# Attention feeding a squared-relu layer: the second state@w_in group of batch 0 moved between the second and third h of the first four

## The chip, the cores and the metric

The kernel runs on one core of one Trainium2 chip. A core has a matmul engine (TensorE, PE in the profile; its weight loads are listed apart as PEld), three engines that compute on vectors (VectorE or DVE, ScalarE or ACT, GpSimd or POOL), an engine that issues transfers (SyncE or SP), and 16 DMA engines that move data. Matmuls write to PSUM, a small memory out of which VectorE or ScalarE copies the results. The metric is the device time of one execution in microseconds (us).

## The reference

Cut to what matters. Eight batches of x (8 heads, 512 tokens, 64 numbers each) and of state (8 heads, 32 slots, 64 numbers each) attend to each other both ways. The result, 544 rows of 512 numbers for each batch, goes through a layer with a squared relu.

```python
# per batch and head: x is 512 x 64, state is 32 x 64
a = softmax(x @ state.T / 8)          # over the 32 slots
xread = a @ state                     # 512 x 64
a2 = softmax(state @ x.T / 8)         # over the 512 tokens
sread = a2 @ x                        # 32 x 64
rows = concat([xread, sread])         # heads side by side: 544 x 512 for each batch

h = rows @ w_in                       # w_in 512 x 2048
r = maximum(h, 0)
g = s * (r * r) + b
out = g @ w_out                       # w_out 2048 x 512, float32
```

The kernel doesn't compute xread. Since (a @ state) @ w_in = a @ (state @ w_in), it forms M = state @ w_in for each head (the small product, with 32 rows for each head) and multiplies it with the shares a. The 2048 columns of h are made in 16 blocks of 128, f = 0 to 15. A block h_f is the sum of two matmuls, g = 0 and g = 1, each over four heads with 32 slots, so 128 rows. M itself is made in four column blocks of 512, c = 0 to 3. Block c is needed by h of f = 4c to 4c + 3.

## The kernel before

The parts that the change and the steps of the prediction touch. `...` marks cuts.

```python
NG = 2                                # heads in two sets, g = 0 and 1
psA = ctx.enter_context(tc.tile_pool(name="psA", bufs=2, space=bass.MemoryType.PSUM))
psH = ctx.enter_context(tc.tile_pool(name="psH", bufs=2, space=bass.MemoryType.PSUM))
psO = ctx.enter_context(tc.tile_pool(name="psO", bufs=2, space=bass.MemoryType.PSUM))
...
def att_M(b, c, how):                 # M = state @ w_in, column block c
    ...
    if how == "split":
        two = [psO.tile([P, FC], FP32, tag="o", name=f"Mps_{b}_{c}_{g}") for g in range(NG)]
    ...
    for q in range(NQ):               # a group: eight matmuls
        for g in range(NG):
            mm(
                two[g][32 * q : 32 * q + 32],
                st_of(b, head_of(g, q), g),
                wi[c][64 * g : 64 * g + 64, q, :],
                tp=(64 * g, 32 * q),
            )
    dst = a["M"][:, :, FC * c : FC * c + FC]
    ...
    elif how == "split":
        nc.vector.tensor_copy(dst[:, 0], two[0])
        (nc.vector.tensor_copy if c in (0, 3) else nc.scalar.copy)(dst[:, 1], two[1])
...
def mm1_open(key, ntok, f):           # PSUM for one h
    pool, tag = psH, "h"
    if key == 0 and f % 2 == 1:
        pool, tag = (psA, "att") if f < 8 else (psH, "h")
    return pool.tile([P, ntok], FP32, tag=tag, name=f"h_{key}_{f}")
...
def mm1_close(key, hps, ntok, f):     # the relu out of PSUM, then the square
    ...
    if key == 0 and f in (1, 3, 5):
        nc.vector.tensor_scalar(r16[:, f % 2], hps, 0.0, None, ALU.max)
        ...
    else:
        nc.scalar.activation(r16[:, f % 2], hps, AF.Relu)
    ...
def mm1_x4(b, f0, between):           # the first four h of batch 0
    hs = [mm1_open(b, S, f0 + i) for i in range(4)]
    for g in range(NG):
        for i in range(4):
            mm1_k(b, f0 + i, g, hs[i])
        if g == 0:
            between()
    for i in range(4):
        mm1_close(b, hs[i], S, f0 + i)
...
with tc.manual_schedule(engines={ET.PE, ET.SP, ET.Pool}):
    ...
    load_wi(0)                        # GpSimd issues: w_in in four column blocks
    load_wi(1)
    ...
    load_wi(2)
    ...
    load_x(1)
    load_wi(3)
    for q in range(4):
        load_wo(q)
    nc.gpsimd.dma_start(out=st16[:, 4:, 0, :], in_=st_v[:, 4:, :])
    load_x(2)
    ...
    att_M(0, 0, "split")              # the first group
    att_D(0, [1])
    warm_up(2)
    mm1_x4(0, 0, lambda: att_M(0, 1, "split"))     # the second group is between()
    ...
    b0 = {
        4: [lambda: att_M(0, 2, "split")],
        9: [lambda: att_xT_pe(1, 0), lambda: att_xT_pe(1, 1), behind_xT],
        10: [lambda: att_T(1, [0, 1])],
        11: [
            lambda: att_M(0, 3, "split"),
            lambda: att_M(1, 0, "dve"),
            lambda: att_D(1, [0, 1]),
        ],
        ...
    }
    for f in range(4, NKF):
        mm1_x(0, f)                   # h of f = 4 to 15, one after the other
        for fn in b0.get(f, []):
            fn()
```

The program of TensorE, SyncE and GpSimd stands in the order in which it is written. A scheduler orders VectorE and ScalarE. In later blocks the kernel loads x4 and x5 at the first and the eighth block of h of batch 2, and it does so before and after the change alike.

Of the kernel before, what the change touches and what calls it, by code (L numbers as in the profile page):

```python
# [14 lines left out]
def kernel(  # L15
# [383 lines left out]
    def mm1_open(key, ntok, f):  # L399
# [4 lines that stand above are left out]
# [9 lines left out]
    def mm1_close(key, hps, ntok, f):  # L413
        if f % 2 == 0:
            pool, tag, n = (apool, "ET", 3) if (key, f) == (0, 0) else (rpool, "r", 3)
            R2[key] = pool.tile([P, 2, ntok], FP16, name=f"r_{key}_{f}", tag=tag, bufs=n)
        r16 = R2[key]
        if key == 0 and f in (1, 3, 5):
            nc.vector.tensor_scalar(r16[:, f % 2], hps, 0.0, None, ALU.max)
            G["last"] = nc.cur_bb.bb.instructions[-1]  # L420
        else:
            nc.scalar.activation(r16[:, f % 2], hps, AF.Relu)  # L422
            G["relu"] = nc.cur_bb.bb.instructions[-1]
        if f % 4 == 0:
            G4[key, f // 4] = gpool.tile([P, 4, ntok], FP16, name=f"g_{key}_{f}", tag="g")
        gt = G4[key, f // 4]
        G[key, f] = gt[:, f % 4]
        if key == 1 and f in (3, 5):
            with tc.issue_after(nc.cur_bb.bb.instructions[-1]):
                nc.scalar.square(gt[:, f % 4 - 1 : f % 4 + 1], r16)  # L430
        elif f % 2 == 1:

            def square():
                nc.vector.tensor_mul(gt[:, f % 4 - 1 : f % 4 + 1], r16, r16)  # L434

            if (key, f) in ((0, 1), (0, 3), (0, 7), (0, 9), (1, 11)):
                held.append(square)
                return
            if (key, f) == (0, 5):
                release(1, 1)  # L440
            square()
            G["last"] = nc.cur_bb.bb.instructions[-1]

    def mm1_k(b, f, g, hps):
        a = A[b]
        mm(
            hps,
            a["M"][:, g, P * f : P * f + P],
            a["a4"][:, g, :],
            start=(g == 0),  # L450
            stop=(g == NG - 1),
        )
# [7 lines left out]
    def mm1_x4(b, f0, between):  # L460
        hs = [mm1_open(b, S, f0 + i) for i in range(4)]
        for g in range(NG):
            for i in range(4):
                mm1_k(b, f0 + i, g, hs[i])
            if g == 0:
                between()
        for i in range(4):
            mm1_close(b, hs[i], S, f0 + i)

# [303 lines left out]
    with tc.manual_schedule(engines={ET.PE, ET.SP, ET.Pool}):  # L773
# [72 lines left out]
        att_D(0, [1])  # L846
        warm_up(2)
        mm1_x4(0, 0, lambda: att_M(0, 1, "split"))

        def behind_xT():  # L850
# [226 lines left out]
```

## Time and profile before

| what | before |
|---|---|
| time, median of 3 runs | 206.67 us (206.36 to 210.62) |
| span of the profiled execution | 204.9 us |
| TensorE busy | 197.8 us |
| VectorE busy | 165.7 us |
| ScalarE busy | 127.5 us |
| GpSimd busy | 38.7 us |
| mean granted TensorE clock | 0.998 |

The span runs from the first to the last instruction. Busy time counts the durations of an engine's instructions; matmuls overlap one another in the pipeline, so that TensorE's is not TensorE at its peak. The chain that ended last follows the work back from the last instruction, at each step to what released it. In the timeline a row merges neighbouring instructions of one kind: start, time from the first start to the last end, engine, line of the kernel, operation, output<-input, and their number. A bracket at a row's end gives the idle time of that engine before it and what ended it.

In the start phase, M<-Mps are the copies of the groups, a<-E,R the shares, h<-a,M the blocks of h, and r<-h their relus. Mps<-wi,stT are the groups themselves. The line L70 is a helper through which all matmuls go. The rows are told apart by their tiles.

### The profile page before, as it was taken

The numbers are of one execution on the slowest core, as the hardware profiler recorded it, in microseconds if no ns is written. First come the engines' busy times: TensorE is split into PE (matmuls) and PEld (weight loads), VectorE is DVE, ScalarE is ACT, GpSimd is POOL, SyncE is SP. The second block draws the span as 40 slices with busy tenths as digits, with TensorE's granted clock in tenths as the row PEclk, the third lists the DMA queues.
The fourth block names the chain that finished last, engine by engine and source line by source line (L and its number), as shares of the span: only waits on it lengthen the run. The fifth ranks groups of instructions, "written<-read, shape, count | busy, mean of one in ns | idle before, by whom it ended". The sixth has DMA issues, their size and how long they took to land.

```text
span 204.9 us, 4900 instructions
## 1 busy us (share of the span) xinstructions
PE 197.8 (97%) x1986; PEld 132.9 (65%) x1986; DVE 165.7 (81%) x301; ACT 127.5 (62%) x253; POOL 38.7 (19%) x66
## 2 busy tenths in 40 slices
PE   7889999999999999999999999999999999999992
PEld 2424333667776776677676767676767777788982
DVE  4589878987969985999679976997699786696862
ACT  2569867899476757765776668666867545543100
POOL 5870001232230231023102101120112012100210
PEclk9999999999999999999999999999999999999999
DMA  5999997999989995939882904160416011200143
GB/s 166 229 203 206 206 194 97 191 122 235 172 116 120 150 290 82 194 98 216 110 102 62 233 25 106 51 163 0 102 54 160 3 51 51 101 6 2 61 147 104
DMA packets 46795, 25.52 MB, mean 125 GB/s; under 512 B 31604, under 2 KB 44788, under 8 KB 46772
## 3 DMA queue, kind: packets, MB, share of 16 engines
q0 software_dynamic: 15568, 16.19, 41.1%
q1 hardware_dynamic: 30324, 8.52, 25.5%
q10 hardware_dynamic: 880, 0.49, 0.9%
q8 instruction: 15, 0.25, 0.5%
q14 instruction: 8, 0.07, 0.1%
HBM read 17.30 MB, written 8.91 MB: 128 GB/s over the span
## 4 chain that ended last, share of the span: by engine, by line
PE 87%; DMA 9%; POOL 1%; DVE 1%; SPq 0%; issue 0%
PE h L70 25%; PE oB L70 18%; PE oA L70 12%; PE oC L70 12%; DMA wi<-in_moe_w_in_dram 6%; PE Mps L70 4%; PE o L70 4%; PE h_sr L70 3%; DMA xf<-in_x_dram 3%; PE oB_0b L70 1%; PE V L70 1%; PE oB_sr L70 1%; PE oC_0b L70 1%; PE oA_0b L70 1%; PE oC_sr L70 1%; PE oA_sr L70 1%
## 5 line engine op out<-in xcount | busy, mean ns | idle before, releaser
L422 ACT ACTIVATE r<-h 128x512 f16<-128x512 f32 x125 | 73.4, 602 | 43.9 <-PE h L70 43.9
L70 PE MATMUL h<-a,M 128*128 128x512 f16 x256 | 73.4, 379 | 0.5 <-ACT r L422 0.3
L70 PEld LDWEIGHTS <-s 128*128 128x128 f16 x464 | 44.1, 98 | 14.8
L434 DVE TENSOR_TENSOR g<-r 128x1024 f16<-128x1024 f16 x62 | 41.9, 681 | 12.4 <-ACT r L422 11.9
L70 PEld LDWEIGHTS <-g 128*128 128x128 f16 x392 | 37.2, 98 | 18.6 <-issue 4.1
L70 PE MATMUL oB<-wd,s 128*128 128x256 f16 x224 | 32.8, 272 | 0.0
L70 PE MATMUL oA<-wo,g 128*128 128x256 f16 x224 | 32.5, 273 | 0.0
L70 PEld LDWEIGHTS <-M 128*128 128x128 f16 x256 | 24.4, 98 | 11.4 <-issue 1.4
L626 POOL DMA_DIRECT2D out_dram<-osb x13 | 8.8, 676 | 69.5 <-DVE rt L352 35.3
L314 ACT CAST M<-Mps 128x1024 f16<-128x1024 f32 x20 | 20.1, 1006 | 0.0
L70 PE MATMUL oC<-wd,s 128*128 128x256 f16 (+1 forms) x120 | 16.5, 266 | 0.0
L70 PE MATMUL oB<-wd,g 128*128 128x256 f16 x112 | 15.7, 273 | 0.0
L70 PE MATMUL oC<-wo,s 128*128 128x256 f16 (+1 forms) x120 | 15.4, 266 | 0.0
L626 POOL DMA_DIRECT2D out_dram<-u x7 | 4.7, 678 | 40.7 <-DVE inv L297 26.6
L422 ACT ACTIVATE r_sr<-h_sr 128x256 f16<-128x256 f32 x16 | 6.1, 382 | 7.9 <-PE h_sr L70 6.4
L653 DVE SCALAR_TENSOR_TENSOR u<-oB,s_bc,qa 128x512 f32<-128x512 f32 x7 | 5.2, 748 | 6.3 <-PE oB L70 6.2
L238 ACT ACTIVATE E<-T 128x256 f16<-128x256 f32 x20 | 7.4, 384 | 4.0 <-PE T L70 4.0
L550 DVE TENSOR_TENSOR s<-s,g 128x1024 f16<-128x1024 f16 x14 | 9.6, 685 | 0.2
L70 PE MATMUL h_sr<-srdT,wi 128*128 128x256 f16 x64 | 9.6, 273 | 0.0
L552 DVE TENSOR_TENSOR s<-g,s 128x1024 f16<-128x1024 f16 x14 | 9.6, 683 | 0.0
L548 DVE TENSOR_TENSOR s<-g,g 128x1024 f16<-128x1024 f16 x14 | 9.5, 682 | 0.0
L543 DVE TENSOR_TENSOR s<-g 128x1024 f16<-128x1024 f16 x14 | 9.5, 683 | 0.0
(137 smaller groups left out, 241.3 us busy)
## 6 DMA issues: line engine op xcount, KB each, us to landing
out_dram<-osb POOLq DMA_DIRECT2D x15, 256.0 KB, 4.2
xn<-in_x_dram POOLq DMA_DIRECT2D x7, 512.0 KB, 8.6
wi<-in_moe_w_in_dram POOLq DMA_DIRECT2D x4, 512.0 KB, 9.3
wo<-in_moe_w_out_dram POOLq DMA_DIRECT2D x4, 512.0 KB, 16.4
out_dram<-u POOLq DMA_DIRECT2D x7, 256.0 KB, 2.5
out_dram<-qb POOLq DMA_DIRECT2D x7, 256.0 KB, 3.2
xf<-in_x_dram SPq DMA_DIRECT2D x2, 512.0 KB, 5.0
out_dram<-osb_0b POOLq DMA_DIRECT2D x2, 128.0 KB, 6.1
```

The lines of the kernel that those rows point to most:

```text
L70: return nc.tensor.matmul(out, lhsT, rhs, start=start, stop=stop, tile_position=tp, is_transpose=is_transpose, skip_group_check=True,)
L238: nc.scalar.activation(a["E"][:, g, 256 * m : 256 * m + 256], Ts[m][:, g, :], AF.Exp, scale=scale, accum_out=a["rs"][:, NG * m + g : NG * ...
L314: nc.scalar.copy(dst, ps)
L422: nc.scalar.activation(r16[:, f % 2], hps, AF.Relu)
L434: nc.vector.tensor_mul(gt[:, f % 4 - 1 : f % 4 + 1], r16, r16)
L543: nc.vector.tensor_sub(o, a11, a21)
L548: nc.vector.tensor_add(o, a21, a22)
L550: nc.vector.tensor_sub(o, SQ[b, 1, j], a11)
L552: nc.vector.tensor_sub(o, a12, SQ[b, 2, j])
L626: nc.gpsimd.dma_start(dst[j][:, :, n0 : n0 + NH], osb)
L653: nc.vector.scalar_tensor_tensor(u, acc["B"], s_bc, kept["qa"], ALU.mult, ALU.add)
```

## The change

The first four blocks of h are made in two halves, g = 0 of all four and g = 1 of all four, with the second group of state@w_in between the halves. The change puts this group between the second and the third h of the half g = 0. It is for the copies of column block 1 out of PSUM, which can begin as soon as the group is done and on which h of f = 4 rests. The number of instructions is the same.

```diff
@@ mm1_x4 @@
         for g in range(NG):
             for i in range(4):
                 mm1_k(b, f0 + i, g, hs[i])
-            if g == 0:
-                between()
+                if (g, i) == (0, 1):
+                    between()
         for i in range(4):
             mm1_close(b, hs[i], S, f0 + i)
```

## The prediction

> **What bounds the kernel now.** I read the page first, then the chain that ended last in order of time, then the timeline of 8 to 24 us, then the landing times of single loads. The page says who is the bound on average:
>
> ```profile
> PE 197.8 (97%) x1986; PEld 132.9 (65%) x1986; DVE 165.7 (81%) x301; ACT 127.5 (62%) x253; POOL 38.7 (19%) x66
> ...
> PE 87%; DMA 9%; POOL 1%; DVE 1%; SPq 0%; issue 0%
> ```
>
> TensorE (PE) carries 87% of the chain, a DMA 9%. The changed instructions run near 13 us, in the start phase, so the average doesn't decide; the chain there does. Its pieces (start, length, what):
>
> ```profile
> 8.04 0.83 POOL xn L121
> 8.87 11.92 DMA wi<-in_moe_w_in_dram
> 20.79 0.04 issue
> 20.83 0.48 PE Mps L70 x8
> 21.31 0.61 DVE M L337
> 21.92 0.68 DVE M L338
> ```
>
> From 8.87 to 20.79 the chain is one transfer: the fourth column block of w_in (wi_3), issued at 8.87 and used by the group of products state@w_in that starts at 20.83. No piece of TensorE between 8.87 and 20.83 lies on it. What the change moves stands inside those 11.92 us:
>
> ```profile
> 11.40 0.41 DVE L281 TENSOR_TENSOR a<-E,R 128x512 f16<-128x512 f16 x1
> ...
> 11.73 0.68 DVE L338 CAST M<-Mps 128x512 f16<-128x512 f32 x1
> ...
> 11.97 1.02 PE L70 MATMUL h<-a,M 128*128 128x512 f16 x4
> 12.39 0.42 DVE L281 TENSOR_TENSOR a<-E,R 128x512 f16<-128x512 f16 x1
> ...
> 12.93 0.41 PE L70 MATMUL Mps<-wi,stT 64*32 64x512 f16 x8
> ...
> 13.27 1.04 PE L70 MATMUL h<-a,M 128*128 128x512 f16 x4
> 13.40 0.69 DVE L337 CAST M<-Mps 128x512 f16<-128x512 f32 x1 [0.58 <-PE Mps L70]
> 13.43 0.59 ACT L338 CAST M<-Mps 128x512 f16<-128x512 f32 x1 [1.07 <-PE Mps L70]
> 13.92 1.09 ACT L422 ACTIVATE r<-h 128x512 f16<-128x512 f32 x2
> 14.01 1.28 DVE L419 TENSOR_SCALAR r<-h 128x512 f16<-128x512 f32 x2
> ...
> 14.57 0.59 PE L70 MATMUL h<-a,M 128*128 128x512 f16 x2 [0.26 <-ACT r L422]
> ```
>
> The first line of h (11.97, four matmuls) is the half g=0 of h0 to h3; then comes the group (12.93), then the half g=1 (13.27). The copies of the group out of PSUM (13.40 on VectorE, 13.43 on ScalarE) are idle before it and wait for it. h4 at 14.57 waits for a relu that frees its buffer.
>
> Then the three places where TensorE meets loads:
>
> ```profile
> 15.09 0.11 PEld L70 LDWEIGHTS <-stT 64*32 64x32 f16 x8 [0.42 <-DMA wi<-in_moe_w_in_dram]
> ...
> 17.44 1.04 PEld L70 LDWEIGHTS <-xn 128*128 128x128 f16 x16 [0.17 <-DMA xn<-in_x_dram]
> ...
> 20.83 0.63 PE L70 MATMUL Mps<-wi,stT 64*32 64x512 f16 x16 [0.24 <-DMA wi<-in_moe_w_in_dram]
> ```
>
> The bracket is idle time of that queue and what released it. Issue starts and times to landing give the landings: wi_1 2.95 + 9.2 = 12.15; wi_2 5.36 + 9.3 = 14.66; x_1 7.99 + 9.4 = 17.39; wi_3 8.87 + 11.9 = 20.77. The 0.42 at 15.09 is hardly a wait: the groups at 12.93 and 26.01 show the same 0.42 with "issue" as cause, and the step from the last h (14.78) is 0.31, as at 12.93 (from 12.62).
>
> **What the Trainium skill says.** "PSUM — Partial Sum Buffer", section Engine vs sequencer instructions: matmuls start and complete in program order, ScalarE and VectorE queues are strict FIFO. So a group that waits holds all matmuls behind it. The trace agrees: nothing of TensorE's work behind wi_3 begins before 20.83. "TensorE: Matmul & The Clock Gate", section Back-to-back issue gap: a single warm matmul of 512 columns costs N/2.4 + 2.5, about 216 ns, though a stream could go to some 131. The trace agrees with the first alone: ten h start at 15.43 and the next matmul at 17.60, 0.217 us each. "DMA: Bandwidth & Descriptors", section Two DMAs through the same engine are not ordered: within one queue of an engine, descriptors start in order. The four landings above come in order of issue, 2.5 to 3.4 us apart, agreeing; compute can't pull wi_3 forward.
>
> **The change part by part.** Nothing is added or removed: the sixteen instructions (eight weight loads and eight matmuls) of the second group pass in front of two matmuls, h2 and h3 of g=0. In the built program only TensorE's order differs; VectorE, ScalarE, GpSimd and SyncE keep theirs, and with it every DMA issue keeps its place. Step by step, before to estimated after:
>
> 1. Group: 12.93 becomes 12.19 (start of h1) + 0.30 (step from an h to a group) = 12.49, 0.44 earlier. It may start: wi_1 landed at 12.15, and its second PSUM half is freed by the VectorE copy ending 11.73 + 0.68 = 12.41, plus 0.06 of signalling (the warm-up matmul started at 11.54 after a copy that ended at 11.48) = 12.47. It fits by 0.02 us.
> 2. h2, h3 of g=0: 12.41 and 12.62 become 12.49 + 0.34 = 12.83 and 13.05. The half g=1 starts at 13.05 + 0.22 = 13.27, as now. TensorE's total is unchanged; only order changes.
> 3. Copies: 13.40 and 13.43 become about 12.96 and 12.99. VectorE is free for it at 12.39 + 0.42 = 12.81.
> 4. Relus: ScalarE's first is freed from the copy (which would end at 13.57) and now waits for h0: 13.27 + 0.38 + 0.06 = 13.71 instead of 13.92, a gain of 0.21. VectorE's first waits for h1: 13.49 + 0.38 + 0.05 = 13.92 instead of 14.01, a gain of 0.09; its second needs h3 at 13.92 + 0.38 and VectorE at 13.92 + 0.68 = 14.60, where it was at 14.61.
> 5. h4 waits for ScalarE's first relu: 13.71 + 0.60 + 0.05 = 14.36 instead of 14.57. So of 0.44 only 0.21 is left on TensorE.
> 6. Third group: 15.09 becomes 14.88, which is after wi_2's 14.66. But the GpSimd issue that waited for the same load began at 14.98; if the load is only then seen, the group starts at 15.0 and the gain is 0.1.
> 7. h5 to h9 then end their ten slots at 17.39 to 17.5, and the transposes of x_1 need it at 17.39; their weight loads start at 17.44 with or without the change. Left: 0.0 to 0.1 on TensorE. ScalarE may keep 0.1 to 0.2 of its relus.
> 8. Fourth group: wi_3 lands at 20.77, the group starts at 20.83. TensorE now idles 0.24 before it and would idle 0.3 to 0.45. Left: 0.0.
>
> Behind 20.83 nothing older is owed: VectorE idled 0.60 before the copy at 21.30, so its backlog is empty, and ScalarE idled 0.19 before D's logarithm at 22.04, itself behind the group. The sum is 0.44 - 0.23 - 0.1 to 0.2 - the rest = 0.0 us. Time: 206.67 - 0.0, within what the runs scatter.
>
> **The rivals.** First, the gain goes through to the end. For it: the idle time at wi_3 is only 0.24, and TensorE has 97% busy time, so any hole filled could seem worth its length. Against it: the hole isn't filled, TensorE's work ahead of 20.83 merely ends sooner and wi_3 doesn't. It would need 206.67 - 0.21 = 206.46, or 206.2 if all 0.44 came through. Second, the group waits. Its margin at the PSUM half is 0.02, and with in-order matmuls a late copy holds h2, h3 and the whole half g=1. For it: the margin is below the accuracy of my step of 0.30. Against it: what could be late is a copy with VectorE continuously busy ahead of it, hence tenths of a us at most, and 0.24 of idle time at wi_3 takes that up. It makes 206.7, and 206.9 if 0.4 were lost. Third, the earlier copies, at 12.96 to 13.65, lie beside GpSimd's issue of the state load (12.54 to 13.61, 1.07 us where a wo load took 0.75). If that issue stretched, the state load and x_2 could shift. Against it: x_2's issue waits until 14.98 for wi_2 anyway, and the state load takes 19.6 us to land behind others. Time 206.6 to 206.8.
>
> **The range and the chances.** The expected effect is zero, so the point is the present time with a slight lean to the first rival: 206.6. Two of the three runs lie 0.31 apart (206.36 and 206.67), the third is at 210.62. A range of 206.2 to 207.1 covers the whole first rival and the second, with the scatter; a time outside needs a moved landing or an odd run. Two per cent is 4.1 us, nearly ten times the largest local effect of 0.44: faster 0.01, same 0.98, slower 0.01.
>
> **What would show it.** In the changed profile the second group starts at 12.45 to 12.6 and its copies near 12.96; the half g=1 stays at 13.27; h4 starts near 14.36; the weight loads of x_1 at 17.44 wait longer than 0.17; the fourth group starts at 20.83 with 0.3 to 0.5 idle before it; and all later groups keep their start times within 0.05. Step 1 is wrong if the group starts with a wait for VectorE. The prediction is wrong if wi_3 lands at another time, or if the start of the fourth group stays and a later group on TensorE still moves by over 0.3 us.

## The result: 207.49 us at first, and no difference in larger sets

| set | kernel before | changed kernel | ratio, 95% interval |
|---|---|---|---|
| first, 4 executions each | 206.68 us median | 207.49 us median (207.31 to 207.72) | 1.0045 (1.0025 to 1.0065) |
| second, 64 and 14 | 207.11 | 207.21 | 0.9994 (0.9969 to 1.0019) |
| third, 59 and 22 | 207.01 | 206.99 | 0.9998 (0.9981 to 1.0016) |

Disturbed executions, such as the one of the kernel before at 210.62, are left out of the ratios but counted in the medians. The first time lies outside the range on record (206.2 to 207.1). The experiments below show why four executions of this kernel tell little: its time has a spread of over 2 us that it owes mostly to one wait, far from the change, in both kernels.

The page of the changed kernel, its busy times and its chain by engine:

```profile
PE 197.2 (96%) x1986; PEld 132.5 (64%) x1986; DVE 165.8 (80%) x301; ACT 127.7 (62%) x253; POOL 38.8 (19%) x66
...
PE 84%; DMA 12%; POOL 1%; DVE 1%; SPq 0%; issue 0%
```

The work is the same; the span is 205.9 us instead of 204.9. The chain has gained 3% of DMA. Where it lies, the chain in order of time tells (start, length, what):

```profile
8.78 11.69 DMA wi<-in_moe_w_in_dram
20.47 0.04 issue
20.52 0.48 PE Mps L70 x8
...
67.65 0.23 PE h L70 x2
67.88 7.09 DMA a<-aT
74.98 0.05 issue
75.02 1.04 PE h L70 x4
```

The fourth group starts 0.31 us earlier than in the first trace of the kernel before, because wi_3 landed earlier. TensorE keeps that lead for 50 us. Then a piece appears that the chain before didn't have: `a<-aT`, the DMA transpose of the softmax shares of batch 3, issued at 67.88 and landed at 74.98. The first h of batch 3 needs it. The kernel before had one and the same place with hardly any wait:

```profile
73.94 0.55 PEld L70 LDWEIGHTS <-M 128*128 128x128 f16 x4 [0.26 <-DMA a<-aT]
```

and the changed kernel at the same place:

```profile
75.02 0.55 PEld L70 LDWEIGHTS <-M 128*128 128x128 f16 x4 [1.67 <-DMA a<-aT]
75.02 1.04 PE L70 MATMUL h<-a,M 128*128 128x512 f16 x4 [1.39 <-DMA a<-aT]
```

Its second line is TensorE itself, which idled 1.39 us there. From 0.3 us ahead to 1.1 us behind: that is the whole difference of the two traces. The question is whether the change brings this wait.

### The profile page after: what moved, and what is told of

Its sections match the earlier page's. It is cut to its first block, busy times and chain, and to the rows that moved or that the text cites. A ratio compares the mean times of both kernels' runs of the same rounds, so it can differ in the third digit from the quotient of the medians.

```text
span 205.9 us, 4900 instructions
## 1 busy us (share of the span) xinstructions
PE 197.2 (96%) x1986; PEld 132.5 (64%) x1986; DVE 165.8 (80%) x301; ACT 127.7 (62%) x253; POOL 38.8 (19%) x66
## 4 chain that ended last, share of the span: by engine, by line
PE 84%; DMA 12%; POOL 1%; DVE 1%; SPq 0%; issue 0%
PE h L70 24%; PE oB L70 18%; PE oC L70 11%; PE oA L70 11%; DMA wi<-in_moe_w_in_dram 6%; PE Mps L70 4%; PE o L70 4%; DMA a<-aT 3%; PE h_sr L70 3%; DMA xf<-in_x_dram 3%; PE oB_0b L70 1%; PE V L70 1%; PE oB_sr L70 1%; PE oC_0b L70 1%; PE oA_0b L70 1%; PE oC_sr L70 1%
```

## The experiments

### The same two kernels once more

No edit: each kernel unchanged, for a second trace.

> The kernel before, unchanged, for a second trace. Theory A (phase at batch 3): the change lets TensorE's program run 0.2 to 0.4 us earlier from the fourth group on, the transpose of batch 3's shares (a<-aT) is then issued 0.3 us earlier into a DMA stall and lands 1 us later, and h of batch 3 waits 1.4 us for it. Here then the transpose is issued at 68.1 to 68.4, lands by 74.1 and h waits under 0.3 us. Theory B (chance): start times and landings differ from one execution to the next as much as between the two kernels; then this trace may show the wait of over 1 us too, and starts at the fourth group that scatter by 0.3 us.

> The changed kernel, unchanged, for a second trace. Theory A: the fourth group again starts 0.2 to 0.4 us earlier than in the kernel before, the transpose of batch 3's shares lands after 74.7 and h waits 1.1 to 1.6 us. Theory B: the wait may be absent, and the fourth group may start as late as 20.8.

Measured: 208.19 us for the kernel before and 208.26 us for the changed one. The kernel before waits too. Its TensorE timeline:

```profile
20.51 0.63 PE L70 MATMUL Mps<-wi,stT 64*32 64x512 f16 x16 [0.41 <-DMA wi<-in_moe_w_in_dram]
...
75.37 0.82 PE L70 MATMUL h<-a,M 128*128 128x512 f16 x3 [1.74 <-DMA a<-aT]
```

So the wait isn't a property of the change. This trace is also the better partner for a comparison of the steps, since TensorE was in the same phase in both (the first h of the four starts at 11.47 in each). The kernel before in that trace:

```profile
11.47 1.02 PE L70 MATMUL h<-a,M 128*128 128x512 f16 x4
...
12.43 0.41 PE L70 MATMUL Mps<-wi,stT 64*32 64x512 f16 x8
...
12.90 0.69 DVE L337 CAST M<-Mps 128x512 f16<-128x512 f32 x1 [0.59 <-PE Mps L70]
12.94 0.58 ACT L338 CAST M<-Mps 128x512 f16<-128x512 f32 x1 [1.08 <-PE Mps L70]
13.42 1.09 ACT L422 ACTIVATE r<-h 128x512 f16<-128x512 f32 x2
13.51 1.28 DVE L419 TENSOR_SCALAR r<-h 128x512 f16<-128x512 f32 x2
...
14.07 0.59 PE L70 MATMUL h<-a,M 128*128 128x512 f16 x2 [0.27 <-ACT r L422]
...
14.60 0.11 PEld L70 LDWEIGHTS <-stT 64*32 64x32 f16 x8 [0.42 <-DMA wi<-in_moe_w_in_dram]
...
17.29 0.90 PEld L70 LDWEIGHTS <-xn 128*128 128x128 f16 x16 [0.52 <-DMA xn<-in_x_dram]
```

and the changed kernel, first trace:

```profile
11.47 0.59 PE L70 MATMUL h<-a,M 128*128 128x512 f16 x2
...
11.99 0.41 PE L70 MATMUL Mps<-wi,stT 64*32 64x512 f16 x8
...
12.46 0.69 DVE L337 CAST M<-Mps 128x512 f16<-128x512 f32 x1
12.50 0.59 ACT L338 CAST M<-Mps 128x512 f16<-128x512 f32 x1 [0.64 <-PE Mps L70]
13.19 1.08 ACT L422 ACTIVATE r<-h 128x512 f16<-128x512 f32 x2
13.41 1.29 DVE L419 TENSOR_SCALAR r<-h 128x512 f16<-128x512 f32 x2 [0.25 <-PE h L70]
13.84 0.10 PEld L70 LDWEIGHTS <-M 128*128 128x128 f16 x1 [0.32 <-issue]
14.44 0.11 PEld L70 LDWEIGHTS <-stT 64*32 64x32 f16 x8 [0.50 <-DMA wi<-in_moe_w_in_dram]
...
17.54 0.90 PEld L70 LDWEIGHTS <-xn 128*128 128x128 f16 x16 [0.93 <-DMA xn<-in_x_dram]
```

The group is 0.44 earlier, its copies 0.44, ScalarE's first relu 0.23, VectorE's 0.10, h4 0.23 (13.84 against 14.07; its first matmul stands inside a longer row, and the weight load of its second starts with it), the third group 0.16 (14.44 against 14.60). Then x_1's landing (weight loads at 17.54 against 17.29) and wi_3's take it all: the fourth group starts at 20.52 and 20.51.

### Work added ahead of the wait

Two matmuls of h of batch 1 are done twice, 0.43 us of TensorE, in the changed kernel and in the kernel before. The doubled product starts its sum anew, so the values are the same.

```diff
         hps = mm1_open(b, S, f)
+        if b == 1 and f in (5, 6):
+            mm1_k(b, f, 0, hps)
         for g in range(NG):
             mm1_k(b, f, g, hps)
```

> The changed kernel with two matmuls of h done twice in batch 1 (f = 5 and 6), 0.43 us more work for TensorE ahead of batch 3. Theory A: everything from there on is 0.43 us later, the transpose is issued near 68.3 as in the kernel before and lands by 74.1, the wait of 1.4 us goes, and the time falls by 0.4 to 0.9 us to 206.6 to 207.1, though work was added. Theory B, or a loss that lies elsewhere: the time rises by up to 0.43 us, to 207.5 to 207.9.

> The kernel before with the same two matmuls doubled, 0.43 us more work. Without any effect of phase: 206.67 + 0.43 = 207.1. Theory A holds no firm number for a later phase than that of the kernel before: 206.9 to 207.3 if the transpose lands 0.4 us later with it, and more if it meets another stall.

Measured: the changed kernel with it 207.27 us median of 12, ratio to the kernel before 1.0006 (0.9979 to 1.0033); the kernel before with it 207.46 of 20, ratio 1.0034 (1.0016 to 1.0053). In both profiled executions the transpose was issued at 68.20 and 68.36, landed after 5.2 and 5.3 us, and h didn't wait; they took 206.53 and 206.66 us. But the other executions scatter from 206.42 to 208.69, as those without the added work do. Neither the median expected by theory A (206.6 to 207.1) nor that of theory B (207.5 to 207.9) came. In the two executions that were profiled the wait was absent at a later phase, and the times don't show that a later phase helps as a rule. The kernel before lost 0.7 us (0.3 to 1.1), which agrees with the 0.43 added; the changed one lost 0.1 us (between a gain of 0.4 and a loss of 0.7), and the two losses can't be told apart.

### Is it the time of issue?

No edit: the changed kernel unchanged, two large sets.

> The changed kernel, unchanged, in many more executions beside the kernel before. Theory A1 (the change has no effect of its own; each execution falls by the landing of wi_3, which scatters from 20.3 to 20.8 us, on the side of batch 3's transpose that waits or on the other, whichever kernel it is): ratio 0.998 to 1.002, times of both from 206.0 to 208.3. Theory A2 (the change makes the early side more likely): ratio 1.002 to 1.005 again.

> The changed kernel, unchanged, a second set beside the kernel before. Equal for both up to the scatter of batch 3's wait: ratio 0.997 to 1.003. If the first four executions (ratio 1.0045) were right after all, 1.003 to 1.006.

Measured: the second and third lines of the table at the top; the change has no effect of its own. The profiled execution of the second set settles a part of theory A. Its timeline at batch 3:

```profile
67.88 1.74 SPq L307 DMA_TRANSPOSE a<-aT  x1
...
73.84 1.04 PE L70 MATMUL h<-a,M 128*128 128x512 f16 x4 [0.21 <-DMA a<-aT]
```

Here the transpose was issued at 67.88 as in the execution with 7.1 us to landing, yet landed after 5.9. So the time of issue doesn't decide, and theory A falls in that point. What the executions share is the company that the transpose keeps. The next runs take it away.

### x5's load moved out of the way

Only the load of x5 moves, in the changed kernel (fifteenth and third block of h of batch 2) and in the kernel before (fifteenth).

```diff
-                at(7, lambda: load_x(5))
+                at(14, lambda: load_x(5))
```

> The changed kernel with x5's load moved from the eighth to the fifteenth block of h of batch 2, behind the transpose of batch 3's shares. Theory A: the transpose of x4 (60 to 72 us) drains without this load beside it, that of the shares lands below 73 us in every phase, h never waits for it: time 206.0 to 206.6, highest below 207.3. Rival C (the stall of all queues at 69.7 to 71.3 us belongs to the transposes, not to the load): landing and wait stay, time 206.7 to 207.7 as in the changed kernel.

> The changed kernel with x5's load at the third block of h of batch 2, ahead of x4's transpose. Theory A: the load is done near 64 instead of 69 us, so the shares' transpose lands 1 to 3 us sooner and the wait goes; time 206.0 to 206.8, unless x5's load delays the write of the batch's outputs, which nothing waits for. Rival C: 206.7 to 207.7.

> The kernel before with the same late load of x5: the place of the second group alone, with the wait of batch 3 out of the way. Prediction's own sum of 0.0 for the change: equal to the changed kernel with the late load within 0.15 us. If the change costs or gains something of its own, they differ by over 0.2 us.

For the third block the number is 2 instead of 14. Then the two with the late load once more, as the first difference (0.14 us between their means, margin 0.13) was at the edge:

> The changed kernel with x5's load at the fifteenth block, a second set. Sum of 0.0 for the change: its mean lies within 0.1 us of that of the kernel before with the same late load (first sets: 206.18 and 206.32, difference -0.14 with a margin of 0.13). If a part of the 0.2 us gained at h4 passes the wait for wi_3, the difference is again -0.1 to -0.2.

> The kernel before with the same late load, a second set: 206.2 to 206.4; equal to the changed kernel with it within 0.1 us if the change is worth 0.0, 0.1 to 0.2 us above it if a part of the gain passes.

| kernel | x5's load | median us (lowest to highest) | ratio, 95% interval |
|---|---|---|---|
| changed | late | 206.14 (205.79 to 206.71) | 0.9957 (0.9940 to 0.9975) |
| changed | early | 206.24 (205.88 to 207.41) | 0.9961 (0.9946 to 0.9977) |
| before | late | 206.33 (205.90 to 206.93) | 0.9963 (0.9950 to 0.9976) |
| changed, second set | late | 206.12 (205.85 to 206.86) | 0.9967 (0.9957 to 0.9978) |
| before, second set | late | 206.13 (205.91 to 207.07) | 0.9960 (0.9944 to 0.9976) |

Three readings. First, the move is worth 0.3 to 0.4% in either direction and in either kernel, and with the late load the spread shrinks from over 2 us to about 1. With the early load three of 22 executions still took 207.25 to 207.41, above the 206.8 expected; no trace of one was kept. Second, the place of the group is worth nothing here either: over both sets the means of the two kernels with the late load differ by 0.06 us with a margin of 0.10. In the second set they differ by 0.02, though the level expected for the kernel before, 206.2 to 206.4, was just missed. Third, the transposes show what the load did. SyncE's issues in the changed kernel, first trace:

```profile
59.77 7.20 SPq L208 DMA_TRANSPOSE xT<-xn  x1
67.88 2.97 SPq L307 DMA_TRANSPOSE a<-aT  x1
```

and with the late load of x5:

```profile
59.72 3.75 SPq L208 DMA_TRANSPOSE xT<-xn  x1
67.82 1.23 SPq L307 DMA_TRANSPOSE a<-aT  x1
```

The transpose of x4, issued at the same time, keeps SyncE for half as long, and that of the shares, again issued at the same time, lands after 3.1 us instead of 7.1. The same holds in all five traces with the load moved (3.6 to 4.1 and 3.1 us), against 6.8 to 7.7 and 5.2 to 7.6 us in all eight with the load at its old place. While x4's transpose runs, from 62 to 64 us, the DMA engines also move less with the load in its old place (the last number of a row is GB/s), in the changed kernel's first trace

```profile
62.00:64.00 2.00, 2.00 (x47) 1.41 (x45) 2.00 (x5) 1.61 (x5) 0.00 (x0) 1.00 0.70 47
```

and with the late load

```profile
62.00:64.00 2.00, 2.00 (x46) 1.41 (x45) 2.00 (x5) 1.61 (x5) 0.00 (x0) 1.00 1.19 203
```

Rival C, for which the load didn't matter, falls. The changed kernel with the late load beats both kernels; so does the kernel before with it, equally.

### What makes up one execution's time

The profiled executions can be added up. Time = start of the fourth group + wait of TensorE for the shares + the rest. Those with added work are left out:

| execution | time us | fourth group | wait | rest |
|---|---|---|---|---|
| before, first | 206.67 | 20.83 | none listed | 185.84 |
| before, again | 208.19 | 20.51 | 1.74 | 185.94 |
| changed, first | 207.72 | 20.52 | 1.39 | 185.81 |
| changed, again | 208.26 | 20.41 | 1.92 | 185.93 |
| changed, second set | 206.50 | 20.50 | 0.21 | 185.79 |
| changed, third set | 206.80 | 20.78 | 0.25 | 185.77 |
| changed, x5 late | 206.09 | 20.38 | 0 | 185.71 |
| changed, x5 early | 206.11 | 20.42 | 0 | 185.69 |
| before, x5 late | 205.90 | 20.25 | 0 | 185.65 |
| changed, x5 late again | 206.68 | 21.04 | 0 | 185.64 |
| before, x5 late again | 206.21 | 20.52 | 0 | 185.69 |

The rest is constant within 0.3 us over times that differ by 2.4. Two terms make the time: when wi_3 lands, and whether the transpose of batch 3 is late. By the sets above, the change moves neither by an amount that shows.

## Why the prediction was right or wrong

Steps 1 to 5 held, by the pair of traces in the same phase: 0.44 at the group (0.44 predicted), no shift of the half g=1 (12.77 before; in the changed kernel 12.78, the third of the eight matmuls of h in a row from 12.33), 0.44 at the copies, 0.23 and 0.10 at the relus (0.21 and 0.09), 0.23 at h4 (0.21). No wait for VectorE's copy appeared ahead of the group: it started 0.31 us after h1 (11.47 + 0.21 = 11.68), the step that the prediction took as 0.30.

Step 6 held at 0.16 (0.1 to 0.21). Step 7 held in kind: the weight loads of x_1 idle 0.93 us in the changed kernel and 0.52 in the kernel before. Step 8 held in its result, 20.52 against 20.51; the idle time ahead of it was 0.25 us and not 0.3 to 0.45, as x_1 had landed 0.25 us later in that execution. The sum of 0.0 for the change is what the two larger sets and the two pairs with the late load measured. What the list of signs got wrong is the start of 20.83 in absolute terms: wi_3's landing scatters between executions, so the group started anywhere from 20.25 to 21.04 over both kernels. One of the prediction's own signs of being wrong, wi_3 landing at another time, came true (20.47 instead of 20.77), and in the second trace of the kernel before the group started as early (20.51).

The step that failed is the range, in its sentence "a time outside needs a moved landing or an odd run". It took the scatter from two executions that lay 0.31 us apart and set the third aside as odd. In the later sets the kernel before runs from 206.0 to 208.9, median 206.9 to 207.1; a range of 206.2 to 207.1 holds about half of its own executions. A moved landing was nothing rare: wi_3's moved by 0.8 us and the wait for batch 3's shares by 1.9 us over the profiled executions of both kernels. The point of 206.6 followed the median of a first set that lay 0.3 to 0.4 below the larger ones.

The second failure lies behind it and could have been seen: the path was followed only to the fourth group, and 1.39 us of the changed kernel's first trace were lost some 54 us later, at the first h of batch 3. "Behind 20.83 nothing older is owed" was right, but I looked for later waits only by what older work was due, not by which later transfers had no slack. The trace before showed one: the weight loads at 73.94 waited 0.26 for a transpose that landed at 73.92. There TensorE arrived at the same moment as a transfer, a place at which both kernels lost more than a microsecond in some executions, and the range should have been open to that side.

The rivals: the full gain didn't come through, the group didn't wait, and the third rival (GpSimd's issue stretched) didn't happen either, 1.07 and 1.08 us in the two traces. None of the three was the event that set the measured number.

One thing stays open. The first ratio, 1.0045, has an interval that doesn't meet those of the larger sets. All four of the changed kernel took 207.3 to 207.7. Chance alone is a poor explanation: in its larger sets 6 of the 31 executions that the ratios count took 207.3 or more, and if executions are independent four of four would come about once in 700. In the order in which they are listed, neighbours in the larger sets of the kernel before aren't alike either (correlation of -0.11 to 0.02). The three later sets ran on three chips, with medians of the kernel before of 206.94, 207.11 and 207.01; on which chip the first set ran isn't on record. So the wait explains the time of the profiled execution, and why the first set fell on its side four times isn't shown.

## What to carry to other kernels

A local gain is worth what is left of it at the next transfer that ends later: follow it from wait to wait until one swallows it. Then look, for the whole program, for places where the bounding engine meets a transfer with no slack, since such places made most of the scatter here, and a difference of 0.4% from four executions each was gone when executions were counted in dozens. To remove such a place, try to keep plain loads away from the DMA transposes that the bounding engine waits for; here moving one load was worth 0.3 to 0.4%, where the reordered matmuls were worth nothing that shows.

## What the runs showed of the hardware that was not expected

Here a DMA transpose lost more beside a plain load than a share of an unchanged rate. From 62 to 64 us the DMA engines moved 45 to 109 GB/s in the eight traces with x5's load beside x4's transpose, and 203 to 245 GB/s in the five with the load moved. x4's transpose held SyncE's queue for 6.8 to 7.7 us with the load and 3.6 to 4.1 without, and the transpose of the shares behind it landed after 5.2 to 7.6 us instead of 3.1. Whether other kinds of transfer do the same wasn't tested.

The DMA packets in the traces also show a standstill. In all eight traces with the load at its old place, 13 to 25 packets of 256 bytes, of the queue with the transposes, opened near 70 us, stayed open for up to 1.5 us and ended within 0.04 us of each other. In the three executions with the long wait, packets of 4 KB of GpSimd's queue then stayed open for some 0.7 us. With the load moved, no packet that opened between 67 and 75 us stayed open longer than 0.84 us. What starts a standstill wasn't tested. In each of the eight a 16 KB packet of the queue that the profile calls "instruction" was open when it began (from 68.8 to 69.9 until 70.3 to 71.0 us); in the five with the load moved it was open between 65.4 and 67.4 us, ahead of the shares' transpose. Moving the load moved this packet too, so which of the two the standstill needs isn't separated. The low rate from 62 to 64 us came before that packet.

The start of the kernel scatters too: the nine warm-up matmuls that begin at 1.19 took 3.4 to 4.0 us, depending on the execution, and the first four h began at 11.97 in one trace of the kernel before and at 11.47 in another.
